# First eight weight slices in memory of their own, unit 0's scans ahead of them, and VectorE's and ScalarE's steps on attention results placed in the next half unit

## The chip, the cores and the metric

The kernel runs on one core of a Trainium2 chip. The engines are TensorE (PE, matmuls), VectorE (DVE), ScalarE (ACT), GpSimd (POOL) and SyncE (SP), which only issues transfers here. Each works through its own instructions in the order in which they were written. The metric is the device time of one execution in microseconds; a lower number is better. Each kernel is timed several times, and the median counts.

## What is computed

A recurrence over 768 positions for 4 x 8 heads of width 48, and two layers behind it:

```python
for t in range(S):
    cur = einsum('bhd,bhe->bhde', u[None] * k[t], v[t])
    y[t] = einsum('bhd,bhde->bhe', r[t], state + cur)
    state = w[t][..., None] * state + einsum('bhd,bhe->bhde', k[t], v[t])
x = y.transpose(0, 2, 1, 3).reshape(3072, 384)
x = ((x @ w1) * (x @ w2) @ w3) @ w_out          # 384 -> 1024 -> 384
h = x @ w_in                                    # 384 -> 2048
out = (h * clip(h + 3, 0, 6) / 6) @ w_out2      # 2048 -> 384
```

The weights come as 64-bit words and are made into float32 on the chip.

## The kernel before

**Attention** is cut into 32 *units* (a batch, one half of the positions, one pair of heads; `m` in the code). A unit is worked in *half units* k, two to a unit. In half 2m stand, in the kernel before, the transposes of k (`do_kn`) and the scores (`do_sc`) on TensorE, GpSimd's and VectorE's preparation of unit m+1 (`prep1`: two scans on VectorE, `e` and `f`, over its `wkr` tile), and at the half's end the mask (`do_mask`). In half 2m+1 stand `do_y(m-1)` and `do_kv(m)` on TensorE, `prep2(m+1)`, the load of unit m+2 (`wkr`, `rkv`; it takes the buffer that `do_y(m-1)` read), and at the end `do_x(m-1)` (VectorE's low part of y, transfers into `xt`), the state's scan and `prep3`. `do_y` ends with a copy on ScalarE. `kt` and `kvs` are ScalarE's copies out of PSUM for `do_kn` and `do_kv`. Three PSUM banks (`abank`) go round among all of these.

**Weights** come in 768 KB *slices*. A slice is loaded, converted in two passes on ScalarE (`a`) and two on VectorE (`b`); those for the first layer (`w12`) and later ones are also split into a high part (ScalarE) and a low part (VectorE) (`c`). `w3` and `w_out` are multiplied ahead of everything in twelve *turns*: turn i needs its own slice of `w3` and, in the first four, one of `w_out`. The matmuls of a turn are line 412; turns 0 to 7 have three groups of them, 8 to 11 two.

**The first layer** works on eight blocks of 384 tokens (`bi`), each in eight *slots* f: `ab(f, 0)` into bank 0, which ScalarE copies out, `ab(f, 1)` into bank 1, their product, the split into gh and gl, and `out1` of the slot before. The layer needs `xt` of the block, that is four units. `mm3` is three matmuls, of high with high, high with low and low with high parts.

**The order** is written out by hand: the engines follow the program's order. `burst(k)` puts the first part of half unit k into a turn or slot and `follow` the second. In the twelve turns half unit k stands in turn k+2. In the first block of the first layer (bi 0) ten half units, 10 to 19, stand in eight slots; f = 2 and f = 5 have two each. Then each slot has one.

Of the kernel before, what the change touches and what calls it, by code (L numbers as in the profile page):

```python
# [23 lines left out]
PR = 112  # L24
# [13 lines left out]
NH = 2 * NM + 2  # L38
# [5 lines left out]
def build(nc, tc, a):  # L44
# [80 lines left out]
    def load(m):  # L125
        wkr = att.tile([PR, WKR], F32, name=f"wkr_{m}", tag="wkr", bufs=3)
        nc.sync.dma_start(wkr, a["wkr"][m])
        rkv = att.tile([128, 3, NC, 2, D], F32, name=f"rkv_{m}", tag="rkv", bufs=3)
        nc.sync.dma_start(rkv, a["rkv"][m])
        un[m] = {"w": wkr[:, :WZ], "k": wkr[:, WZ:WZ + T1], "r": wkr[:, WZ + T1:], "rn": rkv[:, 0], "kn": rkv[:, 1],  # L130
                 "v": rkv[:, 2]}
# [97 lines left out]
    def do_y(m):  # L229
# [18 lines left out]
        y = att.tile([PR, 2, T1], F32R, name=f"y_{m}", tag="y")  # L248
        ACT.copy(y[:, 0], ps)
        d["y"] = y, ps  # L250

    def do_x(m):
        d = un.pop(m)
        b, h, p = m // (2 * NP), (m // NP) % 2, m % NP
        y, ps = d["y"]
# [10 lines left out]
    def attention():  # L266

        for m in range(NM + 1):
            if m < NM:
                do_kn(m)  # L270
                do_sc(m)
            if m + 1 < NM:
                prep1(m + 1)
# [4 lines left out]
            if m > 0:  # L278
                do_y(m - 1)
# [7 lines left out]
            if m > 0:  # L287
# [8 lines left out]
    at_half = [0]  # L296

    def burst(k):

        if at_half[0] == k < NH:  # L300
            next(steps)
            return True
        return False

    def follow(due):
        if due:
            next(steps)
            at_half[0] += 1


    class Slices:


        def __init__(self, bufs):
            self.args, self.raw, self.f, self.bufs, self.loaded = [], {}, {}, bufs, 0

        def load(self, upto):
            while self.loaded < min(upto, len(self.args)):
                key, n, src = self.args[self.loaded][:3]
                t = stg.tile([128, NW, 2], I32, name=f"raw_{key}", tag="raw")  # L320
                self.raw[self.loaded] = t
                nc.sync.dma_start(t[:, :n], src.bitcast(I32).rearrange("p (n t) -> p n t", t=2))
                self.loaded += 1

# [5 lines left out]
        def b(self, i):  # L330
            n, dst = self.args[i][1], self.args[i][3]
            conv_b(self.f[i], self.raw[i][:, :n], False)
            if dst is not None:
                self.load(i + self.bufs + 1)

        def c(self, i):
            dst, f = self.args[i][3], self.f.pop(i).bitcast(F32)
            if dst is not None:
                split(*dst, f)
                return  # L340
            parts = self.raw[i].rearrange("p n t -> p (n t)").bitcast(F32R).rearrange("p (t n) -> p t n", t=2)
            split(parts[:, 0], parts[:, 1], f)
            nc.sync.dma_start(w2d[i - SC], parts.bitcast(F32))
            self.load(i + self.bufs + 1)

    w12p = pool("w12p", bufs=1, side="left")
    w12h = w12p.tile([128, NF1, 2, KT, 128], F32R, name="w12h")
    w12l = w12p.tile([128, NF1, 2, KT, 128], F32R, name="w12l")
    ear = pool("ear", bufs=2, side="left")
    wo = ear.tile([128, NF1, DM], I32, name="wo", bufs=1)  # L350
    sl = Slices(3)
# [15 lines left out]
    sl.args += [(f"w12_{f}", NW, a["w12"][f], (w12h[:, f].rearrange("p s k m -> p (s k m)"),  # L367
                                               w12l[:, f].rearrange("p s k m -> p (s k m)"))) for f in range(NF1)]
# [420 lines left out]
```

## Time and profile before

| | |
|---|---|
| three runs | 926.89, 931.45 and 933.42 us; median 931.45 us |
| profiled execution | 924.55 us, of it 922.8 us from the first to the last instruction |
| TensorE matmuls busy | 866.3 us, 94% of the span |
| VectorE, ScalarE, GpSimd busy | 497.4, 381.0 and 153.0 us |
| mean granted clock of TensorE | 0.979 of full |

A profile is one execution, recorded instruction by instruction. A row of a timeline is an instruction or a run of like ones; behind it, in brackets, the time that the engine stood idle before it and what released it. The names are `output<-input`. L412 is a line of the kernel. TensorE counts two instructions for a matmul of float32 operands.

### The profile page before, as it was taken

To read this page: it belongs to the slowest core of one execution; us is meant where nothing else is said; L and a number is where in the kernel's file an instruction comes from. 1 tells how busy PE (TensorE), PEld (TensorE's weight loads), DVE (VectorE), ACT (ScalarE), POOL (GpSimd) and SP (SyncE) were. 2 spreads that over 40 slices of the span, in tenths; PEclk is the share of its full clock that TensorE was granted. 3 is DMA by queue.
4 is the path that set the end of the run, shared out by engine and by line. 5 is a ranking of instruction groups with operands and counts; after the bars stand their busy time and mean duration, and the time that the engine had idled before them with its cause. 6 is when DMAs were issued, how large, how long until landed. Compare 5 with 4: busy or idle time off the path is not lost.

```text
span 922.8 us, 13198 instructions
## 1 busy us (share of the span) xinstructions
PE 866.3 (94%) x5076; PEld 737.9 (80%) x5076; DVE 497.4 (54%) x783; ACT 381.0 (41%) x885; POOL 153.0 (17%) x186
## 2 busy tenths in 40 slices
PE   3886678999999999999999999999999999999997
PEld 1553567999999999989999788888888888888885
DVE  5876788668687687877433333433334334333332
ACT  4534554445544364444422433433333333333332
POOL 1323243225243443334000000000000000000000
PEclk9998788999999999999999999999999999999999
DMA  8746666255657466665279300100101100000001
GB/s 309 245 131 194 192 212 178 85 176 179 207 181 233 157 204 200 185 211 178 100 291 337 120 1 1 68 1 3 67 0 32 38 1 1 34 1 1 35 0 38
DMA packets 34727, 111.33 MB, mean 121 GB/s; under 512 B 4592, under 2 KB 8032, under 8 KB 34656
## 3 DMA queue, kind: packets, MB, share of 16 engines
q1 hardware_dynamic: 34656, 110.40, 37.1%
q8 instruction: 42, 0.69, 0.3%
q14 instruction: 29, 0.24, 0.1%
HBM read 78.92 MB, written 22.02 MB: 109 GB/s over the span
## 4 chain that ended last, share of the span: by engine, by line
PE 85%; DMA 5%; DVE 5%; issue 2%; ACT 2%; SPq 0%; DVEq 0%; ACTq 0%
PE bank L111 26%; PE bank L112 25%; PE bank L113 24%; PE abank L239 4%; DMA wkr<-in_wkr 3%; PE bank L412 2%; PE abank L194 2%; DMA raw_w<-in_w 1%; DMA xt<-y 1%; PE abank L210 1%; DVE w3f L103 1%; DVE e L146 1%; DVE w3f L104 1%; PE abank L183 1%; ACT sq L165 1%
## 5 line engine op out<-in xcount | busy, mean ns | idle before, releaser
L587 DVE SCALAR_TENSOR_TENSOR q<-q,bank 128x512 f32<-128x512 f32 x96 | 66.1, 688 | 195.2 <-ACT q L586 195.1
L586 ACT ACTIVATE q<-bank,half 128x512 f32<-128x512 f32 x96 | 66.3, 690 | 191.5 <-PE bank L113 191.4
L111 PE MATMUL bank<-xt,w12h 128*128 128x384 f32 x384 | 129.5, 337 | 7.3 <-DMA xt<-y 7.3
L113 PE MATMUL bank<-xt,w12l 128*128 128x384 f32 x384 | 129.0, 336 | 0.0
L112 PE MATMUL bank<-xt,w12h 128*128 128x384 f32 x384 | 128.9, 336 | 0.0
L112 PE MATMUL bank<-x,wih 128*128 128x512 f32 x288 | 114.9, 399 | 0.0
L112 PE MATMUL bank<-gl,w12h 128*128 128x512 f32 x288 | 113.9, 396 | 0.0
L111 PE MATMUL bank<-gh,w12h 128*128 128x512 f32 x288 | 113.7, 395 | 0.0
L111 PE MATMUL bank<-x,wih 128*128 128x512 f32 x288 | 113.5, 394 | 0.0
L113 PE MATMUL bank<-x,wil 128*128 128x512 f32 x288 | 112.8, 392 | 0.0
L113 PE MATMUL bank<-gh,w12l 128*128 128x512 f32 x288 | 112.6, 391 | 0.0
L108 DVE TENSOR_TENSOR gl<-q,gh 128x512 fp32r<-128x512 f32 x96 | 66.6, 693 | 65.5 <-ACT gh L107 65.5
L107 ACT CAST gh<-q 128x512 fp32r<-128x512 f32 x96 | 59.5, 620 | 65.6 <-DVE q L587 65.6
L412 PE MATMUL bank<-wo,w3f 128*128 128x384 f32 x128 | 53.8, 577 | 31.1 <-DVE w3f L104 29.5
L111 PEld LDWEIGHTS bank<-xt,w12h 128*128 128x128 f32 x384 | 72.7, 189 | 7.9 <-DMA xt<-y 7.7
L528 ACT CAST gh<-a 128x384 fp32r<-128x384 f32 x64 | 32.8, 513 | 111.3 <-DVE a L525 111.3
L525 DVE TENSOR_TENSOR a<-a,bank 128x384 f32<-128x384 f32 x64 | 35.3, 552 | 73.8 <-PE bank L113 71.4
L112 PEld LDWEIGHTS bank<-xt,w12h 128*128 128x128 f32 x384 | 72.7, 189 | 0.0
L113 PEld LDWEIGHTS bank<-xt,w12l 128*128 128x128 f32 x384 | 72.6, 189 | 0.0
L111 PE MATMUL bank<-gh,w34h 128*128 128x384 f32 x192 | 71.3, 372 | 0.6 <-ACT gh L528 0.6
L412 PEld LDWEIGHTS bank<-wo,w3f 128*128 128x128 f32 x128 | 27.5, 223 | 51.6 <-DVE w3f L104 31.3
L173 POOL TENSOR_SCALAR_AFFINE_SELECT A<-sd 128x384 f32<-128x384 f32 x64 | 50.0, 805 | 108.0 <-DVE sd L170 62.9
(101 smaller groups left out, 1491.2 us busy)
## 6 DMA issues: line engine op xcount, KB each, us to landing
wkr<-in_wkr SPq DMA_DIRECT2D x32, 505.8 KB, 5.5
rkv<-in_rkv SPq DMA_DIRECT2D x32, 432.0 KB, 6.3
raw_w<-in_w SPq DMA_DIRECT2D x16, 768.0 KB, 4.9
xt<-y SPq DMA_DIRECT2D x48, 144.0 KB, 5.2
raw_w_in<-in_w_in SPq DMA_DIRECT2D x8, 768.0 KB, 5.0
w2d<-raw_w_in SPq DMA_DIRECT2D x8, 768.0 KB, 3.3
raw_w_out<-in_w_out SPq DMA_DIRECT2D x8, 768.0 KB, 4.9
w2d<-raw_w_out SPq DMA_DIRECT2D x8, 768.0 KB, 3.3
```

Of the source, the lines that this page charges most:

```text
L107: ACT.copy(hi, src)
L108: (eng or V).tensor_tensor(out=lo, in0=src, in1=hi.bitcast(F32), op=ALU.subtract)
L111: mm(ps, wh, xh, start=first, stop=False)
L112: mm(ps, wh, xl, start=False, stop=False)
L113: mm(ps, wl, xh, start=False, stop=last)
L173: P_.affine_select(out=A[:, j], in_=sd[:, :, j].unsqueeze(2).to_broadcast([128, NC, C]), pattern=[[0, NC], [-1, C]], compare_op=ALU.is_equ ...
L239: mm(pc[rows[j], c], left, right, start=not started[j], stop=True, skip_group_check=True)
L412: mm(bank[g % 5][:, :DM], w3[:, j, g - g0], wo[:, 2 * jp + j].bitcast(F32), start=jp + j == 0, stop=jp == NF1 // 2 - 1 and j == 1)
L525: V.tensor_tensor(out=at, in0=at, in1=bank[1][:, :T1], op=ALU.mult)
L528: ACT.copy(gh, at)
L586: ACT.activation(q, ps, AF.Relu, bias=half, scale=1.0 / 6.0)
L587: V.scalar_tensor_tensor(out=q, in0=q, scalar=1.0, in1=ps, op0=ALU.min, op1=ALU.mult)
```

## The change

1. The first eight slices (`w_out` 0 to 3 and `w3` 0 to 3) get tiles of their own (`homes`), in the memory in which the first layer's weights `w12h` and `w12l` are made at turn 9. All eleven slices up to `w3` 6 are asked for at the start. The converted `wo` and `w3f` tiles move to the other side of the memory.
2. Unit 0's `wkr` is loaded first of all and its scans are put ahead of the first slice. Slice 1 and the constants are issued from ScalarE's queue.
3. A half unit now begins with `follow(k)`, which holds what works on TensorE's results of the half before: at the start of half 2m the copy of y, `do_x(m-2)` and the state's scan of unit m-1, at the start of half 2m+1 the mask of unit m. `prep3` moves to half 2m. There are 67 half units instead of 66.
4. Half unit k stands in turn k+1 instead of k+2. In the first block nine half units, 11 to 19, stand in eight slots, two of them in f = 3.
5. The high part of a split slice is cast behind its conversion (`b`) instead of with the low part; the low parts of the first two `w12` slices come a turn later. In a turn, the passes of `a` stand ahead of `b`.

```diff
     def attention():
 
-        for m in range(NM + 1):
+        for m in range(NM + 2):
+            if m > 1:
+                do_x(m - 2)
+            if 0 < m <= NM:
+                do_state(m - 1)
+            yield
             if m < NM:
                 do_kn(m)
                 do_sc(m)
+            if 0 < m < NM:
+                prep3(m)
             if m + 1 < NM:
                 prep1(m + 1)
             yield
             if m < NM:
                 do_mask(m)
             yield
...
-            if m > 0:
-                do_x(m - 1)
-            if m < NM:
-                do_state(m)
-            if m + 1 < NM:
-                prep3(m + 1)
-            yield
...
+    def follow(k):
         if at_half[0] == k < NH:
             next(steps)
+            at_half[0] += 1
+
+    def burst(k):
+        follow(k)
+        if at_half[1] == k < NH:
             next(steps)
-            at_half[0] += 1
+            at_half[1] += 1
...
                 key, n, src = self.args[self.loaded][:3]
-                t = stg.tile([128, NW, 2], I32, name=f"raw_{key}", tag="raw")
+                if self.loaded < len(self.homes):
+                    t = self.homes[self.loaded]
+                else:
+                    t = stg.tile([128, NW, 2], I32, name=f"raw_{key}", tag="raw")
...
             if dst is not None:
...
+            ACT.copy(dst[0], self.f[i].bitcast(F32))
...
+    load(0, 0)
+    ACT.dma_start(d1c, a["d1c"])
     sl.load(2)
-    nc.sync.dma_start(d1c, a["d1c"])
-    load(0)
+    load(0, 1)
     for nm, t in (("u", ub), ("ident", ident), ("mask", mask)):
-        nc.sync.dma_start(t, a[nm])
-    sl.load(3)
+        ACT.dma_start(t, a[nm])
+    sl.load(4)
     load(1)
+    sl.load(len(homes) + 3)
...
         for f in range(NF1):
+            k = NF1 * bi + f + LEAD - (bi == 0 and f < 4)
+            if bi or f:
+                follow(k)
...
-            k = NF1 * bi + f + LEAD - (2 if f < 3 else 1 if f < 6 else 0) * (bi == 0)
-            due = burst(k)
+            burst(k)
```

The copy of y also moves in the code, from the end of `do_y` to the start of `do_x`.

**SyncE's queue at the start.** `home` and `raw_w3` are slices, `wkr` and `rkv` are what a unit loads. Before:

```order
L322 DMA raw_wo_1_131<-in_w_out 128x1536
L127 DMA wkr_1_133<-in_wkr 112x1156
L129 DMA rkv_1_135<-in_rkv 128x864
L322 DMA raw_w3_1_156<-in_w3 128x1536
L322 DMA raw_wo_2_160<-in_w_out 128x1536
L322 DMA raw_w3_2_183<-in_w3 128x1536
L322 DMA raw_wo_3_187<-in_w_out 128x1536
L322 DMA raw_w3_3_216<-in_w3 128x1536
L322 DMA raw_w3_4_220<-in_w3 128x1536
L322 DMA raw_w3_5_254<-in_w3 128x1536
L322 DMA raw_w3_6_258<-in_w3 128x1536
L127 DMA wkr_2_288<-in_wkr 112x1156
```

After:

```order
L329 DMA home2_115<-in_w_out 128x1536
L329 DMA home3_116<-in_w3 128x1536
L128 DMA wkr_1_137<-in_wkr 112x1156
L132 DMA rkv_1_139<-in_rkv 128x864
L329 DMA home4_117<-in_w_out 128x1536
L329 DMA home5_118<-in_w3 128x1536
L329 DMA home6_119<-in_w_out 128x1536
L329 DMA home7_120<-in_w3 128x1536
L329 DMA raw_w3_4_145<-in_w3 128x1536
L329 DMA raw_w3_5_147<-in_w3 128x1536
L329 DMA raw_w3_6_149<-in_w3 128x1536
L128 DMA wkr_2_273<-in_wkr 112x1156
```

The slices that waited for a buffer now stand in one row, and unit 2's `wkr` behind eleven of them (one is issued from ScalarE).

**ScalarE, turn 5 before and turns 4 and 5 after.** `w3f_7` and `w3f_6` are the slices of the turn after next, `y_0` the copy of unit 0's result. Before:

```order
L249 CAST y_0_363<-abank2_69 112x384
L215 COPY kvs1_99<-abank0_67 112x48x3
L162 COPY pb0_100<-e_2_332 112x48x3
L165 ACTIVATE sq_2_0_376,stat_74<-wkr_2_288 112x128
L165 ACTIVATE sq_2_1_378,stat_74<-wkr_2_288 112x128
L165 ACTIVATE sq_2_2_380,stat_74<-wkr_2_288 112x128
L94 ACTIVATE w3f_7_390,sums_77<-raw_w3_7_294 128x768
L96 ACTIVATE raw_w3_7_294<-raw_w3_7_294 128x768
L185 COPY kt_2_414<-abank1_68 128x336
L148 COPY stat_74<-d1v1_97 112x3
```

After:

```order
L217 COPY kvs1_99<-abank0_67 112x48x3
L164 COPY pb0_100<-e_2_311 112x48x3
L167 ACTIVATE sq_2_0_359,stat_74<-wkr_2_273 112x128
L167 ACTIVATE sq_2_1_361,stat_74<-wkr_2_273 112x128
L167 ACTIVATE sq_2_2_363,stat_74<-wkr_2_273 112x128
L94 ACTIVATE w3f_6_369,sums_77<-raw_w3_6_149 128x768
L96 ACTIVATE raw_w3_6_149<-raw_w3_6_149 128x768
L257 CAST y_0_382<-abank2_69 112x384
L187 COPY kt_2_394<-abank1_68 128x336
L150 COPY stat_74<-d1v1_97 112x3
```

The copy of y has moved behind kvs, pb, the squares and the two passes over a slice.

**TensorE, first block of the first layer.** `abank` are the banks of attention; before, in slot f = 2, where units 5 and 6 meet (the same stands at f = 5 for units 7 and 8):

```order
L183 MATMUL abank0_67<-ident_73,wkr_6_662 128x112 x2
L194 MATMUL abank1_68<-wkr_6_662 128x128
L194 MATMUL abank2_69<-wkr_6_662 128x128
L194 MATMUL abank1_68<-wkr_6_662 128x128
L194 MATMUL abank2_69<-wkr_6_662 128x128
L194 MATMUL abank1_68<-wkr_6_662 128x128
L194 MATMUL abank2_69<-wkr_6_662 128x128
L239 MATMUL abank0_67<-wkr_5_568,s_5_821 48x128 x6
L239 MATMUL abank0_67<-A_5_680,rkv_5_570 48x128 x6
L210 MATMUL abank1_68<-rkv_6_664,kt_6_870 48x48 x4
```

After, in slot f = 3, where units 6 and 7 meet:

```order
L185 MATMUL abank2_69<-ident_73,wkr_7_779 128x112 x2
L196 MATMUL abank0_67<-wkr_7_779 128x128
L196 MATMUL abank1_68<-wkr_7_779 128x128
L196 MATMUL abank0_67<-wkr_7_779 128x128
L196 MATMUL abank1_68<-wkr_7_779 128x128
L196 MATMUL abank0_67<-wkr_7_779 128x128
L196 MATMUL abank1_68<-wkr_7_779 128x128
L241 MATMUL abank2_69<-wkr_6_647,s_6_941 48x128 x6
L241 MATMUL abank2_69<-A_6_837,rkv_6_649 48x128 x6
L212 MATMUL abank0_67<-rkv_7_781,kt_7_977 48x48 x4
```

Two places at which half units stand directly behind one another have become one.

## Rows read from the trace of the kernel before

**Rows 1.** Windows; columns: length, busy us of each engine (instructions), clock, DMA share, GB/s

```profile
105.92:173.40 67.48, 58.10 (x438) 53.38 (x439) 50.65 (x82) 30.88 (x88) 18.62 (x23) 0.87 0.51 152
...
155.00:460.00 305.00, 302.54 (x2378) 284.28 (x2375) 223.13 (x372) 146.19 (x430) 108.39 (x128) 0.99 0.57 176
```

**Rows 2.** What TensorE waited for; columns: us in total, times, longest us

```profile
PE bank L412 <- DVE w3f L104: 29.5, 7, 11.2
PE bank L111 <- DMA xt<-y: 7.3, 1, 7.3
PE abank L239 <- ACT kt L185: 5.8, 2, 3.3
```

**Rows 3.** Chain that ended last, stretch 49 to 65 us; start, us, what

```profile
54.52 3.88 DMA wkr<-in_wkr
...
58.49 0.98 DVE e L146
...
61.55 0.97 DVE w3f L104
```

**Rows 4.** DMA issues: KB each, median us to landing

```profile
wkr<-in_wkr SPq DMA_DIRECT2D x32, 505.8 KB, 5.5
...
raw_w<-in_w SPq DMA_DIRECT2D x16, 768.0 KB, 4.9
```

**Rows 5.** Windows over the first 20 us, columns as in Rows 1

```profile
0.00:10.00 10.00, 0.00 (x0) 0.00 (x0) 4.97 (x9) 4.85 (x7) 1.54 (x10) 1.00 0.80 263
10.00:20.00 10.00, 7.11 (x12) 3.64 (x12) 5.28 (x7) 2.69 (x6) 2.89 (x2) 1.00 1.03 366
```

**Rows 6.** Timeline of ScalarE; start us, us, instruction, [idle before <-releaser]

```profile
55.33 0.48 ACT L249 CAST y<-abank 112x384 fp32r<-112x384 f32 x1 [7.00 <-PE abank L239]
...
55.70 0.29 ACT L215 COPY kvs<-abank 112x144 f32<-112x144 f32 x1
...
58.17 0.90 ACT L96 ACTIVATE raw_w<-raw_w 128x768 int32<-128x768 uint8 x1
...
100.73 0.82 ACT L107 CAST w12h<-f_w 128x768 fp32r<-128x768 f32 x1
```

**Rows 7.** Timeline of VectorE, columns as in Rows 6

```profile
55.84 0.56 DVE L256 TENSOR_TENSOR y<-abank,y 112x384 fp32r<-112x384 f32 x1 [2.42 <-ACT y L249]
...
56.88 0.43 DVE L170 TENSOR_REDUCE sd<-rkv 128x6 f32<-128x288 f32 x1
...
101.58 0.96 DVE L108 TENSOR_TENSOR w12l<-f_w,w12h 128x768 fp32r<-128x768 f32 x1 [1.41 <-ACT w12h L107]
```

**Rows 8.** Timeline of TensorE, turns 4, 5, 9 and 10

```profile
39.76 2.85 PE L412 MATMUL bank<-wo,w3f 128*128 128x384 f32 x8
...
49.74 4.14 PE L412 MATMUL bank<-wo,w3f 128*128 128x384 f32 x12 [2.81 <-DVE w3f L104]
...
55.11 0.44 PE L210 MATMUL abank<-rkv,kt 128*48 128x48 f32 x12
...
77.22 5.26 PE L412 MATMUL bank<-wo,w3f 128*128 128x384 f32 x8 [4.91 <-DVE w3f L104]
...
84.08 2.85 PE L412 MATMUL bank<-wo,w3f 128*128 128x384 f32 x8
```

**Rows 9.** Windows behind the two waits for kt, and one at full clock

```profile
126.11:133.49 7.38, 6.15 (x42) 5.26 (x43) 7.31 (x13) 4.16 (x14) 3.24 (x3) 0.54 0.76 244
...
142.65:146.14 3.49, 3.49 (x42) 3.29 (x42) 2.84 (x6) 1.95 (x8) 0.00 (x0) 1.00 0.36 117
...
153.12:160.76 7.64, 6.04 (x46) 5.27 (x46) 6.67 (x12) 3.00 (x11) 4.27 (x6) 0.55 0.79 240
```

**Rows 10.** Timelines of ScalarE, VectorE and TensorE in one slot

```profile
181.20 0.48 ACT L523 COPY a<-bank 128x384 f32<-128x384 f32 x1 [1.08 <-PE bank L113]
...
181.93 0.96 DVE L104 SCALAR_TENSOR_TENSOR f_w_in<-raw_w_in,f_w_in 128x768 int32<-128x768 int32 x1
...
186.00 0.33 PE L111 MATMUL bank<-xt,w12h 128*128 128x384 f32 x1
```

More of the change, by code (lines that the diff above doesn't have):

```diff
@@ L123, in psum_a, with load @@
         return abank[nbank[0] % 3]
[L125 to L131, printed above, removed]
+    def load(m, part=None):
+        if part != 1:
+            wkr = att.tile([PR, WKR], F32, name=f"wkr_{m}", tag="wkr", bufs=3)
+            nc.sync.dma_start(wkr, a["wkr"][m])
+            un[m] = {"w": wkr[:, :WZ], "k": wkr[:, WZ:WZ + T1], "r": wkr[:, WZ + T1:]}
+        if part != 0:
+            rkv = att.tile([128, 3, NC, 2, D], F32, name=f"rkv_{m}", tag="rkv", bufs=3)
+            nc.sync.dma_start(rkv, a["rkv"][m])
+            un[m].update(rn=rkv[:, 0], kn=rkv[:, 1], v=rkv[:, 2])
     def c3(x):
@@ L247, in do_y @@
                 part(j, c, d["v"][:, c, j], d["A"][:, j, c])
[L248 to L250 removed]
+        d["y"] = ps
     def do_x(m):
@@ L254, in do_x @@
         b, h, p = m // (2 * NP), (m // NP) % 2, m % NP
-        y, ps = d["y"]
+        ps = d["y"]
+        y = att.tile([PR, 2, T1], F32R, name=f"y_{m}", tag="y")
+        ACT.copy(y[:, 0], ps)
         V.tensor_tensor(out=y[:, 1], in0=ps, in1=y[:, 0].bitcast(F32), op=ALU.subtract)
@@ L366, in build @@
     S12 = len(sl.args)
-    sl.args += [(f"w12_{f}", NW, a["w12"][f], (w12h[:, f].rearrange("p s k m -> p (s k m)"),
-                                               w12l[:, f].rearrange("p s k m -> p (s k m)"))) for f in range(NF1)]
+    sl.args += [(f"w12_{f}", NW, a["w12"][f], f) for f in range(NF1)]
     SC = len(sl.args)
@@ L397, in w34_part @@
             split(w34h[:, g], w34l[:, g], bank[g % 5][:, :DM])
+    w12 = []
+    prep1(0)
     for q in of[0]:
@@ L421, in build @@
         else:
-            burst(i - 2)
+            burst(i - 1)
+        if i + 2 < len(turns):
+            for q in of[i + 2]:
+                sl.a(q)
+        if i == 9:
+            close("hm")
+            w12p = pool("w12p", bufs=1, side="left")
+            w12 += [w12p.tile([128, NF1, 2, KT, 128], F32R, name=f"w12{x}") for x in "hl"]
+        if i >= 9:
+            sl.a(S12 + i - 9)
         if i + 1 < len(turns):
@@ L427, in build @@
             sl.b(S12 + i - 10)
-        if i + 2 < len(turns):
-            for q in of[i + 2]:
-                sl.a(q)
-        if i >= 9:
-            sl.a(S12 + i - 9)
-        follow(i > 1)
-        if i >= 10:
-            sl.c(S12 + i - 10)
+        if i >= 11:
+            sl.c(S12 + i - 11)
+    sl.c(S12 + 1)
     w34_part((6, 7))
     close("ear")
+    w12h, w12l = w12
     x1p = pool("x1p", bufs=1, side="left")
@@ L538, in build @@
                 step += 1
-            follow(due)
-            if bi == 0 and f in (2, 5):
-                follow(burst(k + 1))
+            if bi == 0 and f == 3:
+                burst(k + 1)
             if prev is not None:
@@ L544, in build @@
             prev = bi, f, gh, gl
-            if bi == 6 and at_half[0] == NH and "h" not in p2:
+            if bi == 6 and at_half[1] == NH and "h" not in p2:
                 win_start()
```

56 lines of the change are left out of this document (30 added, 26 removed).

## Prediction

> **What bounds the kernel now.** I read first the busy time by stage [rows 1]. From 155 to 460 us TensorE works 302.5 of 305 us, so in the long middle no wait is left for a change of order to remove. In the first layer's first block of tokens (105.9 to 173.4 us) it works 58.1 of 67.5 us, and part of that at a low clock. So what can be won lies before 173 us. Then I read who made TensorE wait [rows 2]: the converted weight slices of the twelve turns (29.5 us in 7 waits), the one transfer of attention output into `xt` ahead of the first layer (7.3 us) and ScalarE's copy of `kt` (two waits, 5.8 us), which is where two half units stand directly behind one another. These three are what the change touches. The rest of this part of the program is a chain over two turns: matmuls of turn i, `do_y` and `do_kv` behind them, then either a load of `wkr` or ScalarE's work, then VectorE's two scans and its conversion of the slice for turn i+2, then the matmuls of turn i+2 [rows 3].
>
> The sum is made against the profiled execution, 924.55 us (span 922.8 and 1.75 around it). It is 6.9 us below the median of the runs shown (931.45), and they spread over 6.5 us; so a difference under about 1% (9.3 us) is hardly told from none here.
>
> **Up to turn 4.** Slices now wait for no buffer until the twelfth, so the queue is full from the start, and bytes decide. Ahead of unit 2's `wkr` now stand eleven slices of 768 KB, two earlier `wkr` [rows 4], and by their shapes 0.9 MB of `rkv` and 0.5 MB of constants; with `wkr` 2 itself that is 8.65 + 1.55 + 0.9 + 0.5 = 11.6 MB. The transfers moved 263 GB/s in the first 10 us and 366 GB/s in the next 10 [rows 5]. At these rates 2.6 MB are there at 10 us and the other 9.0 MB take 24.5 us: `wkr` 2 lands at 34.5 us. Behind it VectorE runs unit 2's scans and the conversion of turn 4's slice. In the trace from the scan at 58.49 to the end of the conversion at 62.5 this is 4.0 us [rows 3]. So turn 4 starts at 38.5 us; before it was 39.8 [rows 8]. VectorE itself doesn't set it: by then it has 9 slices at 1.95, three pairs of scans at 2.1 and some 4 us of smaller work, 28 us from about 5 on. The scans of unit 0 ahead of the first slice cost their 2.1 us at the first matmul alone and are caught up in that wait. If the queue kept 263 GB/s, `wkr` 2 would land at 44.2; I take 366, the row of the ten microseconds in which the queue was as full as it now will be. So up to here the gain is 1.3 us, but the attention stands one half unit further.
>
> **From turn 4 to the first layer.** The order on VectorE is cyclically the old one. On ScalarE it isn't: `do_x`'s copy of y stood ahead of kvs, pb and squares; now it stands behind them and behind the first pass over the slice of turn i+2. So x, the state scan, the reduction and the next scans wait for it. By rows, a new loop over two turns is: matmuls, y and kv 5.8 (49.74 to 55.55) [rows 8]; to ScalarE 0.2; kvs, pb, squares and the slice 3.4 (55.70 to 59.07), y 0.5 [rows 6]; from x to the end of the reduction 1.5 [rows 7]; scans and conversion 4.0. That is 15.4 us. The old loop went over the load (3.9 us from 54.52) [rows 3] and took 12.8 at the same place: the new one is 2.5 us longer. Turns 4 to 6 and 6 to 8 cost 15.4 each. Turns 8 to 10 have two groups of matmuls instead of three (2.85 us instead of 4.14) [rows 8]: 14.1. Slices there are a third narrower too; what that saves I leave uncounted, against conversions that run longer beside GpSimd's work. From turn 10 to the first layer the conversion's high part (0.8) [rows 6] and low part (0.9) [rows 7] of the first w12 slice come on top: 15.8. Together 60.7 us. In each loop TensorE has work for about 11 of 15 us, so one wait of some 4 us is left per loop. A wait of 2.81 us left the twelve matmuls behind it at 4.14 us, which is full speed; one of 4.91 us was followed by 5.26 us where 2.85 is usual [rows 8]. The new waits are nearer to the second, so I add 2.4 us for each of three loops, 7.2.
>
> The Trainium skill (TensorE: Matmul & The Clock Gate, section "HAM oscillation — how this bites in real kernels") tells of a loop in which one wait per turn drops the clock so that every turn starts at the lower level, and advises another order of the loop. The two rows bear that out for the longer wait and not for the shorter; by that rule all three loops pay and the sum stays, by the row of 2.81 us none pays and the end would be 7.2 us earlier. It speaks against this change, which gathers the waits.
>
> So the first layer's third matmul, the first that needs the low part, comes at 38.5 + 60.7 + 7.2 = 106.4. Before, six matmuls ran ahead of the wait for `xt` and the seventh came at about 105.9. Now four more matmuls stand behind it, 0.7 us. The wait for `xt` (7.3) is gone, since y of unit 3 is out one turn earlier, but what is late next is that low part on VectorE. Net: 1.2 us later than before.
>
> **The first block of the first layer.** Before, unit 6's two halves stand directly behind one another and unit 8's again: the half with `do_y` must wait for `kt`, `do_kv` for the mask. The two waits for `kt` are 5.8 us [rows 2]; in the stretches behind them TensorE stood another 1.23 and 1.60 us (7.38 less 6.15, 7.64 less 6.04), and its granted clock was 0.54 and 0.55 of full, nearly always the lower of its two levels (1.2 of 2.4 GHz) [rows 9]. Work of the same kind at full clock takes 3.49 us there, so the clock cost 2.7 and 2.5 us. In all 13.8 us for two places. After the change one such place is left, at f = 3. I cost it at half, 6.9, and win 6.9. The half unit that moved ahead of the layer takes about 1 us of matmuls with it; against it stands that ScalarE's copy of bank 0 now queues behind the cast of the high part, which waits for VectorE. I set these two against each other. VectorE keeps up: it was busy 50.7 of 67.5 us [rows 1] and gets one half unit less.
>
> **Later.** The half units run one place earlier or later beside the same tiles, and TensorE is full; the end of attention is tied to the same y, so layer 2 finds its weights as before. I count nothing.
>
> Sum: 1.2 - 6.9 = -5.7 us, 919 in a profile like the one shown, and 931.45 - 5.7, about 926, beside the median.
>
> **Rivals.**
> - *The gathered waits are cheap.* If they come out under 3 us, the clock stays up: 7.2 us less, -12.9, 918.6. For it: the row of 2.81; narrower slices shorten the last loops. Against it: the sum leaves about 4 us.
> - *The front is late.* All early transfers now share the engines at once; if they move 310 GB/s on average instead of 366, `wkr` 2 lands at 39 and turn 4 starts at 43. Nothing later takes up those 4.5 us, as the loops are chains. -1.2 us, 930. For it: only one ten-microsecond row shows 366. Against it: that row is the fullest.
> - *Slower: the cast in front of bank 0.* In every slot that converts a slice (6 in the first block, 16 later), ScalarE's cast of the high part now stands ahead of the copy that frees bank 0, and waits for VectorE's conversion. In the slot at 180 us the copy ran at 181.20, the conversion ended at 182.89, and bank 0 was needed again at 186.00 [rows 10]. The copy would now end at 182.9 + 0.8 + 0.5 = 184.2, 1.8 us in time. From a conversion that ends over 1.8 us later on TensorE waits, microsecond for microsecond, where it now never does. At 1 us in each of 22 slots this is +22, so +16 in all: 948. For it: VectorE is busy 223 of 305 us there [rows 1], and its work comes in lumps. Against it: the slack, which grows in slots without a lump.
> - *Another double place instead.* If the place at f = 3 costs as much as both did (as masks now stand ahead of it), the sum is +1.2: 933.
>
> **Chances.** Forecast (-9 to -2) 0.48; cheap waits 0.22; late front 0.15; double place 0.07; cast 0.08. Faster by over 1% (below 922.1) takes most of the cheap waits and the forecast's lower edge: 0.33. Slower by over 1% (above 940.8) is the cast: 0.08. The rest, 0.59, is within 1%. The range reaches from the cheap waits with a good front (-17, 914) to the late front or the double place (933), and leaves out the cast and the tail below.
>
> **What would show it.** First matmul at 13 to 14 us instead of 11.2; turn 4 near 39 us with unit 2's scans released by its `wkr`; from turn 4 on VectorE idle ahead of x, released by ScalarE's copy of y, 4 to 6 us a time; waits of TensorE of about 4 us before turns 6, 8 and 10 with a low granted clock behind them; no wait for `xt`, but one for the low part of the first slice; one wait for `kt` instead of two. It would be wrong if turn 4 came after 43 us, if bank 0 appeared among TensorE's waits after 175 us, or if the loops took no longer than 13 us.

## The result, and the profile after

The changed kernel takes 920.49 us (median of 4 runs, 918.39 to 920.89), the kernel before beside it 929.39 (4 runs, 926.89 to 933.42): ratio 0.9896, 95% interval 0.9851 to 0.9940. The forecast was 926 with a range of 914 to 933. The profiled execution took 918.39 us with a span of 916.7, against 924.55 and 922.8 before: 6.1 us less, where the sum had said 5.7. The medians are further apart, 8.9 us: in the twenty executions of the kernel before that were timed beside E1 to E4, time and granted clock go together (924.58 us at 0.979, 934.80 us at 0.967), and the profiled one (924.55 us at 0.979) is among the shortest. So the account below explains the 6.1 us of two profiles; where the other 3 us of the medians lie isn't shown. The first tile of the second block of tokens, (1,0), begins at 166.76 instead of 173.38, 6.6 us earlier, and from there to the end the changed kernel takes 749.9 us and the one before 749.4. So all of the 6.1 us was won ahead of 167 us, as forecast; but the steps didn't each give what the sum said.

What TensorE waited for, after (us in total, times, longest):

```profile
PE bank L436 <- DVE w3f L104: 29.3, 7, 16.5
PE bank L113 <- DVE w12l L363: 4.2, 1, 4.2
PE abank L241 <- ACT kt L187: 4.1, 1, 4.1
PE abank L196 <- DVE y L258: 2.9, 2, 2.1
PE bank L111 <- ACT a L553: 2.2, 2, 1.9
PE abank L212 <- DVE A L202: 2.0, 4, 0.8
```

Beside [rows 2], the wait for `xt` (7.3) is gone, and one wait for `kt` is left instead of two. New are the low part of the first w12 slice (4.2) and bank 0, which ScalarE's copy frees too late (2.2); the wait for VectorE's part of y, 0.7 before, is 2.9. The converted slices cost as much as before, 29.3 against 29.5, though 16.5 of it is now the start.

Rows picked from the timeline of TensorE after: the first matmul, turns 4, 6, 8, 10, the third matmul of the first layer, and two places in the first block:

```profile
16.53 10.44 PE L436 MATMUL bank<-wo,w3f 128*128 128x384 f32 x24 [16.53 <-DVE w3f L104]
39.78 4.14 PE L436 MATMUL bank<-wo,w3f 128*128 128x384 f32 x12
55.00 5.83 PE L436 MATMUL bank<-wo,w3f 128*128 128x384 f32 x12 [2.80 <-DVE w3f L104]
70.93 2.85 PE L436 MATMUL bank<-wo,w3f 128*128 128x384 f32 x8 [3.20 <-DVE w3f L104]
83.87 5.49 PE L436 MATMUL bank<-wo,w3f 128*128 128x384 f32 x8 [3.56 <-DVE w3f L104]
102.67 0.69 PE L113 MATMUL bank<-xt,w12l 128*128 128x384 f32 x1 [4.23 <-DVE w12l L363]
125.38 0.44 PE L111 MATMUL bank<-xt,w12h 128*128 128x384 f32 x1 [1.93 <-ACT a L553]
134.03 1.52 PE L241 MATMUL abank<-wkr,s 48*48 48x128 f32 x12 [4.09 <-ACT kt L187]
```

Windows after, columns as in [rows 1]: the first block, the double place, and the matmuls of turns 6, 10 and 8:

```profile
102.67:166.76 64.09, 56.76 (x428) 51.36 (x428) 52.49 (x81) 31.98 (x91) 23.10 (x23) 0.91 0.55 171
134.03:141.50 7.47, 6.64 (x43) 5.71 (x44) 6.67 (x12) 3.20 (x13) 5.24 (x5) 0.54 0.56 177
55.00:60.83 5.83, 5.83 (x14) 3.00 (x14) 4.19 (x6) 0.00 (x0) 1.53 (x3) 0.71 0.27 90
83.87:89.36 5.49, 5.49 (x10) 2.59 (x11) 5.42 (x8) 1.00 (x3) 1.95 (x3) 0.50 0.40 143
70.93:73.78 2.85, 2.85 (x10) 1.51 (x12) 2.85 (x7) 0.00 (x1) 1.53 (x3) 1.00 0.50 171
```

Read both together: turn 6 at a granted clock of 0.71 and turn 10 at 0.50, the lower level, pay 1.7 and 2.6 us over the 4.14 and 2.85 of full clock. Turn 8, behind a wait between the two in length, pays nothing in this execution; in E2 and E4 below it does.

VectorE after: the first conversion, the scan that opens unit 2, and the four places where it waits for y:

```profile
11.58 0.96 DVE L103 SCALAR_TENSOR_TENSOR wo<-wo,home 128x768 int32<-128x768 int32 x1 [2.73 <-ACT home L96]
35.33 0.96 DVE L148 TENSOR_TENSOR_SCAN e<-wkr,d1c 112x388 f32<-112x388 f32 x1
49.36 0.56 DVE L258 TENSOR_TENSOR y<-abank,y 112x384 fp32r<-112x384 f32 x1 [2.51 <-ACT y L257]
65.82 0.56 DVE L258 TENSOR_TENSOR y<-abank,y 112x384 fp32r<-112x384 f32 x1 [6.59 <-ACT y L257]
78.76 0.56 DVE L258 TENSOR_TENSOR y<-abank,y 112x384 fp32r<-112x384 f32 x1 [3.30 <-ACT y L257]
95.56 0.56 DVE L258 TENSOR_TENSOR y<-abank,y 112x384 fp32r<-112x384 f32 x1 [6.11 <-ACT y L257]
```

The scan at 35.33 has no idle time before it: `wkr` 2 was there, and from 11.58 to 39.5 VectorE runs without a gap. The last four rows are the stall that the prediction put into its loops. ScalarE after, from the matmuls' end to y, and the cast in front of bank 0's copy:

```profile
62.55 0.28 ACT L217 COPY kvs<-abank 112x144 f32<-112x144 f32 x1 [8.71 <-PE abank L212]
...
64.78 0.65 ACT L96 ACTIVATE raw_w<-raw_w 128x512 int32<-128x512 uint8 x1
65.33 0.46 ACT L257 CAST y<-abank 112x384 fp32r<-112x384 f32 x1
...
124.12 0.83 ACT L355 CAST w12h<-f_w 128x768 fp32r<-128x768 f32 x1 [4.06 <-DVE f_w L104]
124.86 0.47 ACT L553 COPY a<-bank 128x384 f32<-128x384 f32 x1
```

Between the matmuls' end (62.5) and the copy of y (65.33) ScalarE does 2.8 us of other work, while VectorE stands; of the 6.59 us that it stood, about half fall into this time, and the rest ahead of the matmuls' end. And the cast at 124.12 waited 4.06 us for VectorE with the copy of bank 0 behind it.

### The profile page after: what moved, and what is told of

Its sections match the earlier page's. It is cut to its first block, busy times and chain, and to the rows that moved or that the text cites. A ratio compares the mean times of both kernels' runs of the same rounds, so it can differ in the third digit from the quotient of the medians.

```text
span 916.7 us, 13158 instructions
## 1 busy us (share of the span) xinstructions
PE 863.8 (94%) x5076; PEld 736.0 (80%) x5076; DVE 497.9 (54%) x783; ACT 380.6 (42%) x885; POOL 173.3 (19%) x186
## 4 chain that ended last, share of the span: by engine, by line
PE 85%; DVE 7%; ACT 3%; DMA 3%; issue 1%; SPq 0%; DVEq 0%; ACTq 0%
PE bank L111 26%; PE bank L112 25%; PE bank L113 24%; PE abank L241 5%; PE abank L196 2%; PE bank L436 2%; DMA wkr<-in_wkr 2%; DMA home<-in_w 1%; PE abank L212 1%; DVE e L148 1%; ACT sq L167 1%; DVE w3f L103 1%; PE abank L185 1%; DVE A L202 1%; DVE f_w L104 1%
## 5 line engine op out<-in xcount | busy, mean ns | idle before, releaser
L175 POOL TENSOR_SCALAR_AFFINE_SELECT A<-sd 128x384 f32<-128x384 f32 x64 | 84.0, 1334 | 146.1 <-DVE sd L172 70.8
L436 PE MATMUL bank<-wo,w3f 128*128 128x384 f32 x128 | 51.0, 554 | 29.4 <-DVE w3f L104 29.3
L112 PE MATMUL bank<-gl,w34h 128*128 128x384 f32 x192 | 65.0, 339 | 0.5 <-DVE gl L560 0.5
```

What stands on the lines that cost most here:

```text
L112: mm(ps, wh, xl, start=False, stop=False)
L175: P_.affine_select(out=A[:, j], in_=sd[:, :, j].unsqueeze(2).to_broadcast([128, NC, C]), pattern=[[0, NC], [-1, C]], compare_op=ALU.is_equ ...
L436: mm(bank[g % 5][:, :DM], w3[:, j, g - g0], wo[:, 2 * jp + j].bitcast(F32), start=jp + j == 0, stop=jp == NF1 // 2 - 1 and j == 1)
```

## The experiments

Every kernel of the experiments was timed in five rounds beside the kernel before; the ratios are against it (that of the changed kernel is the one above). "Low part" is the start of the first layer's third matmul (before, and in E3, where the wait stands at `xt`: the matmul behind that wait), (1,0) the start of the second block's first tile ("half unit (1,0)" in the expectations), all in us of one profiled execution each.

```
kernel                          turn 4  low part   (1,0)   span   ratio (95% interval)
before                           39.76   105.92   173.38   922.8
after                            39.78   102.67   166.76   916.7  0.9896 (0.9851 to 0.9940)
E3  front alone                  36.67   103.58   170.76   920.6  0.9963 (0.9943 to 0.9983)
E2  without homes                41.13   104.53   169.57   918.9  0.9938 (0.9912 to 0.9963)
E1  y early                      39.55    94.60   159.29   909.0  0.9798 (0.9769 to 0.9827)
E4  double place later           40.70   104.04   168.11   917.1  0.9893 (0.9863 to 0.9923)
E8  matmuls in the waits         39.20    99.46   164.56   914.1  0.9840 (0.9806 to 0.9873)
E5  y early, cast late           39.26    96.89   156.37   906.5  0.9751 (0.9716 to 0.9787)
E6  y early, one queue           37.86    94.69   159.35   909.7  0.9802 (0.9764 to 0.9840)
E9  y early, low part first      39.48    91.58   159.68   908.9  0.9795 (0.9759 to 0.9831)
E10 four edits                   40.78    95.02   155.45   905.6  0.9736 (0.9704 to 0.9768)
E11 E10, low part first, xt      38.85    90.53   154.34   904.5  0.9736 (0.9711 to 0.9761)
E14 y early, double at f = 6     39.77    94.97   158.71   909.5  0.9783 (0.9761 to 0.9806)
E15 E11, double at f = 6         37.75    89.58   152.20   902.6  0.9713 (0.9684 to 0.9742)
```

From (1,0) to the end of the span all fourteen lie between 749.0 and 750.8 us: whatever is won stands at (1,0).

**E3, front alone, and E2, without homes.** E3 is the kernel before with the front of the change (homes, unit 0's scans first, ScalarE's queue). 

> The kernel before with the front of the change alone: eight slices into the first layer's memory, unit 0's scans first, slice 1 and the constants from ScalarE's queue; the half units stay where they were, with y's copy in do_y. Theory (the gain sits in the first block, where one double place is left instead of two): turn 4 starts at 39 to 41 us as in both kernels, since VectorE sets it; the two waits for kt (5.8 us) and the wait for xt (7.3 us) stay; the first block begins and ends as before, 167 to 175 us for half unit (1,0); time against the kernel before 0.995 to 1.003, that is, of the gain of 1.0% at most a half. Rival (the front is what wins, since no loop waits for a load of wkr any more): each of the loops is 2 to 4 us shorter than before, the first layer begins 6 us or more earlier, ratio 0.985 to 0.992.

E2 is the changed kernel without the homes:

```
-    homes = [hm.tile([128, NW, 2], I32, name=f"home{q}") for q in range(8)]
+    homes = []
...
-    sl.load(4)
+    sl.load(3)
     load(1)
-    sl.load(len(homes) + 3)
```

and with the second passes of turn i+1 ahead of the first passes of turn i+2. 

> The changed kernel with its half units where the change places them, but without the eight slices in the first layer's memory: three buffers as before, and each turn's first pass ahead of the one after it, as the buffers need it. Theory (the placement wins in the first block; the front only keeps the loads away from the loops): the loops wait for wkr again, up to 4 us in one or two of them, the third matmul of the first layer comes 2 to 6 us later than in the changed kernel (102.7), from there to half unit (1,0) it takes 62 to 65 us as in the changed kernel; ratio against the kernel before 0.990 to 0.998. Rival (the front wins, the placement gives nothing): 0.998 to 1.005. Second rival (the slices in the first layer's memory give nothing at all): 0.988 to 0.991, as the changed kernel.

At (1,0) E3 wins 2.6 us on before and E2 3.8: together 6.4, and the change has 6.6. Both keep unit 0's scans first and ScalarE's queue, so the split isn't clean, but neither half needs the other. The placement looks the larger; the intervals of the two ratios overlap. In E3 turn 4 comes at 36.67, not at 39 to 41 as expected: there the attention is a half unit less far and VectorE has less ahead of it. Its waits for `xt` (6.7) and `kt` (two, 5.8 in all) stay as in [rows 2]. In E2 the loops do not wait for `wkr` again, against the expectation; from turn 4 to the low part they take 63.4 us, as after (62.9). By one profile each, the homes, with that order of passes, are worth 1.35 us at turn 4 and 2.8 at (1,0); 1.5 of the 2.8 is turn 8, which ran at the lower clock in E2 (4.39 us instead of 2.85), and by ratio E2 and the changed kernel aren't told apart.

**E1, y early.** The copy goes back to the end of `do_y`, and `do_x` takes both tiles from there:

```
-        d["y"] = ps
+        y = att.tile([PR, 2, T1], F32R, name=f"y_{m}", tag="y")
+        ACT.copy(y[:, 0], ps)
+        d["y"] = y, ps
...
-        ps = d["y"]
-        y = att.tile([PR, 2, T1], F32R, name=f"y_{m}", tag="y")
-        ACT.copy(y[:, 0], ps)
+        y, ps = d["y"]
```

> The changed kernel with ScalarE's copy of y back at the end of do_y, as before the change; all else as changed. Theory (the copy of y behind kvs, pb, squares and a slice's pass lengthens each loop over two turns, and TensorE pays in waits before turns 6, 8 and 10 and in the lower clock behind them): VectorE's idle time ahead of x falls from 2.5 to 6.6 us to under 1.5 us a time, the loops shrink by 1 to 3 us each, the third matmul of the first layer comes 4 to 8 us before 102.7; ratio against the kernel before 0.981 to 0.986. Rival (something else is late next in the loop: kvs and pb, which now stand behind the copy, or the slices on VectorE): the loops stay within 0.5 us each, ratio 0.988 to 0.991. Second rival (the copy waits for the last matmuls of do_y and holds ScalarE's queue): slower than the changed kernel, 0.991 to 0.996.

The low part comes 8.1 us earlier and the span is 7.7 us shorter, more than expected. E1's VectorE and TensorE, where after had 6.59 and 6.11 idle, 15.93 between turns 6 and 8, and 18.80 from turn 10 to the low part:

```profile
60.07 0.56 DVE L258 TENSOR_TENSOR y<-abank,y 112x384 fp32r<-112x384 f32 x1 [2.42 <-ACT y L251]
...
85.68 0.56 DVE L258 TENSOR_TENSOR y<-abank,y 112x384 fp32r<-112x384 f32 x1 [1.50 <-ACT y L251]
```

```profile
53.97 4.14 PE L436 MATMUL bank<-wo,w3f 128*128 128x384 f32 x12 [2.00 <-DVE w3f L104]
67.01 2.85 PE L436 MATMUL bank<-wo,w3f 128*128 128x384 f32 x8 [2.00 <-DVE w3f L104]
79.18 4.54 PE L436 MATMUL bank<-wo,w3f 128*128 128x384 f32 x8 [3.67 <-DVE w3f L104]
94.60 0.69 PE L113 MATMUL bank<-xt,w12l 128*128 128x384 f32 x1 [4.36 <-DVE w12l L363]
```

The four stretches from turn 4 to the low part are 14.42, 13.04, 12.17 and 15.42 us, against 15.22, 15.93, 12.94 and 18.80: the place of one copy of 0.46 us cost the changed kernel 7.8 us, through VectorE's idle time and, at turns 6 and 10, through the clock.

**E8, matmuls in the waits.** It asks whether the clock is a cost of its own:

```
         w3 = w3s.pop(i).bitcast(F32).rearrange("p (j g m) -> p j g m", j=2, m=128)
+        for q in range(6 if i in (6, 8, 10) else 0):
+            mm(bank[3 if i == 10 else 2][:, :DM], wo[:, 0, :128].bitcast(F32), wo[:, 1].bitcast(F32), start=True, stop=True)
```

> The changed kernel with six more matmuls ahead of turns 6, 8 and 10 each, whose results nobody reads: they stand in the places where TensorE waits 2.8, 3.2 and 3.6 us for a converted slice, and fill 2.1 us of each (six of 0.35 us). Nothing else is changed. Theory (the lower clock behind those waits is a cost of its own, beside the wait): turns 6 and 10 run at 4.14 and 2.85 us instead of 5.83 and 5.49, the third matmul of the first layer comes 2 to 5 us before 102.7; ratio against the kernel before 0.984 to 0.988. Rival (the low clock costs nothing, since VectorE and ScalarE set the loop and the next wait only grows): turns 6 and 10 at full speed, but the next waits longer by as much, 0.988 to 0.991. Second rival (the fillers delay the slices' matmuls or don't keep the clock): 0.989 to 0.995.

```profile
55.55 4.03 PE L438 MATMUL bank<-wo,w3f 128*128 128x384 f32 x12
70.38 2.74 PE L438 MATMUL bank<-wo,w3f 128*128 128x384 f32 x8
83.56 2.74 PE L438 MATMUL bank<-wo,w3f 128*128 128x384 f32 x8
```

All three turns run at full clock (granted 1.00). One such matmul is two instructions, so six took 4.14 us and not 2.1: turn 6 now starts 16.35 us behind turn 4 instead of 15.22. Yet the low part comes 3.2 us earlier, 0.6 of which is from ahead of turn 4; the other 2.6 are the clock's, net of that delay. So the low clock is a cost beside the wait. Matmuls that compute nothing paid for themselves, though six were more than the waits held.

**E4, the double place later.**

```
-            if bi == 0 and f == 3:
-                burst(k + 1)
             if prev is not None:
                 out1(*prev)
+            if bi == 0 and f == 3:
+                burst(k + 1)
```

> The changed kernel with the second half unit of f = 3 in the first block placed behind out1 of the tile before instead of ahead of it. Theory (the last double place costs its wait for kt of 4.1 us, 0.8 us for the mask and the low clock behind): the wait for kt falls under 1 us, the stretch from the third matmul to half unit (1,0) shrinks by 2 to 5 us; ratio against the kernel before 0.984 to 0.988. Rival (what comes behind it is late anyway, or the pair of out1 and half unit now delays bank 0's product): the stretch stays within 1 us, ratio 0.988 to 0.991.

```profile
135.35 0.90 PE L241 MATMUL abank<-wkr,s 48*48 48x128 f32 x12 [0.85 <-ACT kt L187]
...
139.15 0.56 PE L212 MATMUL abank<-rkv,kt 128*48 128x48 f32 x8 [2.11 <-DVE A L202]
```

The wait for `kt` fell from 4.09 to 0.85, and the one for the mask grew from 0.83 to 2.11; from the low part to (1,0) it is 64.07 us, after 64.09. The wait fell as the theory said, but the stretch stayed, as the rival said: a wait was moved, nothing won.

**E5, the cast behind bank 0's copy**, on E1. In the slots of the first layer that convert a slice, `b` leaves the cast out and the slot does it behind the copy:

```
             ACT.copy(at, bank[0][:, :T1])
+            if bi == 0 and f + 2 < NF1:
+                sl.high(S12 + f + 2)
+            elif bi and step < 3 * NF2 and step % 3 == 1:
+                sl.high(SC + step // 3)
             ab(f, 1, x)
```

> The changed kernel with y's copy early (0.980 of the kernel before), and with ScalarE's cast of a slice's high part behind its copy of bank 0 instead of ahead of it, in every slot of the first layer that converts a slice. Theory (ahead of the copy, the cast waits for VectorE and holds bank 0: TensorE's wait of 1.9 us in the first block is its cost, and later there is slack): that wait goes, ratio 0.977 to 0.979 if nothing else is late, the long middle unchanged. Rival (VectorE's own lateness is the cause, the wait only goes to the next operation, gh or the low part): 0.979 to 0.982. Second rival (the cast in front costs in later slots too): under 0.976.

The wait for bank 0 is gone, and the first block shrinks by more than that wait: from the low part to (1,0) 59.48 us instead of E1's 64.69. Its low part came 2.3 us later than E1's, with turns 8 and 10 at the lower clock, so 2.9 of these 5.2 us reach (1,0). The later low part isn't what shortens the block: from the start of tile f = 1 to that of f = 5, the seven kernels with the cast in front and the double place at f = 3 take 37.11 to 38.76 us, whenever their low part comes, and E5, E10 and E11, with the cast behind, 33.55 to 34.49. The ratio is the one of the second rival (under 0.976), but not for its reason. E1 and E5 take the same from (1,0) on (749.7 and 750.1): in the later slots the cast in front costs nothing.

**E6, one queue**, on E1: `nc.sync` instead of `ACT` issues slice 1, d1c and the constants. 

> The changed kernel with y's copy early (0.980 of the kernel before), and with slice 1, d1c and the constants issued from SyncE's queue in the same order as before the change of queue, ScalarE issuing none. Theory (VectorE is busy without a gap from 11.6 us to turn 4, so the start of its first slice sets turn 4, and the transfer of d1c and slice 1 on a second queue takes bandwidth from slice 0): slice 0 lands 1 to 2.5 us earlier, the first matmul comes at 13.5 to 15.5 instead of 16.3, turn 4 at 37.5 to 39 instead of 39.6, and the end by as much: ratio 0.9775 to 0.979. Rival (turn 4 waits for something else as well, or the loops take it up at a load of wkr): first matmul earlier, end the same, 0.979 to 0.981. Second rival (one queue is slower, as SyncE issues one after another): first matmul later than 16.3, over 0.981.

The first rival's ratio came out, but not its cause. The first pass over slice 0 starts at 7.27 instead of 9.56, the first matmul comes at 13.99 instead of 16.29 and turn 4 1.7 us earlier. No load takes that up: turn 6 still starts 2.4 us ahead of E1's. Then turns 6 and 8 fall to the lower clock (granted 0.71 and 0.62), which no rival had named, and give it back:

```profile
51.58 5.83 PE L436 MATMUL bank<-wo,w3f 128*128 128x384 f32 x12 [1.88 <-DVE w3f L104]
...
65.81 4.54 PE L436 MATMUL bank<-wo,w3f 128*128 128x384 f32 x8 [1.50 <-DVE w3f L104]
```

**E9, the low part first**, on E1: `sl.c(S12 + i - 11)` moves ahead of `sl.b(S12 + i - 10)`. 

> The changed kernel with y's copy early (0.980 of the kernel before), and with the low part of the first w12 slice ahead of the conversion of the second on VectorE, in the last turn. Theory (TensorE's wait of 4.4 us for the low part is VectorE's order: the part's input is there at 89.6 us, but scans of 2.5 us and a conversion of 2.4 us stand ahead of it): the third matmul of the first layer comes at 92 to 92.7 instead of 94.6; then xt (0.3 us behind in the run before) or the second tile is next, so of the 2.2 us some 1 to 2 reach the end: ratio 0.978 to 0.979. Rival (the conversion that is now later delays the second tile by as much): 0.9795 to 0.981.

```profile
91.58 0.44 PE L113 MATMUL bank<-xt,w12l 128*128 128x384 f32 x1 [1.57 <-DVE w12l L363]
96.30 0.66 PE L111 MATMUL bank<-xt,w12h 128*128 128x384 f32 x1 [3.60 <-DMA xt<-y]
```

The wait for the low part fell from 4.36 to 1.57, and `xt`, hidden behind it until then, is late next with 3.60; (1,0) doesn't move. The rival's ratio came out, though what ate the gain was `xt` and not the second tile.

**E10, four edits; E11, two more.** E10 joins E1, E5, E6 and fewer matmuls in the waits, `range({6: 2, 8: 2, 10: 4}.get(i, 0))`. 

> The changed kernel with four edits together: y's copy early, the cast behind bank 0's copy, one queue for the first transfers, and matmuls without a reader in the waits of turns 6, 8 and 10, fewer than in the run with fillers alone (two of 0.69 us at turns 6 and 8, four at turn 10, as the waits with y early are 1.5 to 2.1 and 3.7 to 4.0 us). Theory (with the clock kept up, the 1.7 us that one queue gave at turn 4 and the 1.7 us of the cast reach the end): turn 4 at 37.5 to 38.2, turns 6, 8 and 10 at 4.14, 2.85 and 2.85 us, half unit (1,0) begins 3 to 5 us before 159.3, ratio 0.970 to 0.975 against 0.980 with y early alone. Rival (the loops are set by loads of wkr and by VectorE, the end stays): 0.975 to 0.979. Second rival (the fillers delay the turns): over 0.979.

Turns 6, 8 and 10 run at 4.14, 2.85 and 2.85. Turn 4 came later than expected, since VectorE here waited 1.83 us for unit 2's `wkr`:

```profile
35.89 0.97 DVE L148 TENSOR_TENSOR_SCAN e<-wkr,d1c 112x388 f32<-112x388 f32 x1 [1.83 <-DMA wkr<-in_wkr]
```

With VectorE started earlier, that transfer is next, though not by as much in every execution: E6, E11 and E15, with the same front, waited 0.28, 0.64 and 0.27 us there. Turn 4 itself ran at the lower clock (granted 0.71, 5.83 us). The profiled execution, 907.39 us, is 2.5 us above the median of its six runs, so the late turn 4 need not be in all of them. The ratio is as the theory said, but E5 alone has 0.9751: what one queue and the matmuls in the waits add to it isn't told from nothing.

E11 adds E9's edit and, for the last unit of the first `xt`, `(ACT if m == NP - 1 else nc.sync).dma_start`. 

> As the kernel with four edits, and two more: the low part of the first w12 slice ahead of the conversion of the second, and the last two transfers of y into the first xt issued from ScalarE's queue instead of SyncE's. Theory (with the low part early, TensorE waited 3.6 us for xt in the run before; that transfer took 9.4 us from its issue because 2.5 MB of loads stood ahead of it on its queue): on a queue of its own it lands in 4 to 6 us, the wait for xt falls under 1 us, and 2 to 4 us more reach half unit (1,0): ratio 0.966 to 0.972. Rival (all queues share the same engines, the transfer takes as long as before): the wait stays 2 to 4 us and the end that of the four edits. Second rival (ScalarE waits for y's low part on VectorE and holds the next operations): later than with four edits.

Transfers of y into `xt` (KB each, median us to landing), in E9 and then in E11, from 78 and 76 to 100 us:

```profile
xt<-y SPq DMA_DIRECT2D x2, 144.0 KB, 9.4
```

```profile
xt<-y ACTq DMA_DIRECT2D x2, 144.0 KB, 6.5
```

The transfer is shorter (in E10, on SyncE's queue, it took 8.5 us), if not the 4 to 6 us of the theory, and `xt` is waited for no more. In its place stand the low part again (3.85) and bank 0, which is read out for the last `w34` blocks (2.35). (1,0) comes 1.1 us earlier than in E10, and the ratio is that of E10, as the first rival had it.

**E14, the double place at f = 6**, on E1, and **E15**, the same on E11. 

> The changed kernel with y's copy early (0.980 of the kernel before), and the one remaining double place moved from f = 3 to f = 6 of the first block, behind the last conversion of a slice. Theory (the double place costs what it costs because VectorE has a slice's conversion between its two halves, so that mask, kt and the next y come late): at f = 6 the waits for kt and the mask are under 2 us in all instead of 4.7, the clock stays up, the stretch from the third matmul to half unit (1,0) shrinks by 2 to 5 us of its 64.7; ratio 0.974 to 0.978. Rival (two half units behind one another always cost about 5 us, wherever they stand): the stretch within 1 us of 64.7, 0.979 to 0.981. Second rival (unit 7's x now comes too late for the second block): a wait for xt at (1,0) of some us, 0.979 to 0.985.

> As the kernel with the four edits, the low part first and xt from ScalarE's queue (0.974 of the kernel before), with the double place moved from f = 3 to f = 6 as well. Theory (at f = 6 the wait for kt went, but ScalarE's copy of bank 0, behind a cast that waits for VectorE, took its place with 4.6 us; with the cast behind the copy that isn't there): no wait for kt, bank 0's waits under 0.5 us, the stretch from the third matmul to half unit (1,0) is 59 to 61.5 us instead of 63.8, ratio 0.969 to 0.972. Rival (VectorE's conversions and half units set the stretch, so another operation is late in their place): 62.5 to 64.5 us, ratio 0.973 to 0.975.

```
-            k = NF1 * bi + f + LEAD - (bi == 0 and f < 4)
+            k = NF1 * bi + f + LEAD - (bi == 0 and f < 7)
...
-            if bi == 0 and f == 3:
+            if bi == 0 and f == 6:
```

E14's waits for bank 0, which were 1.9 us in E1:

```profile
PE bank L111 <- ACT a L553: 4.6, 3, 1.9
```

The wait for `kt` is gone (3.9 in E1), and bank 0 took its place; from the low part to (1,0) it is 63.74, 1 us less, as the first rival had it; the ratio lies between the two ranges. In E15 neither is there; the mask (1.6), y (1.4) and the scanned `wkr` (0.9) are, each a VectorE product, and the stretch is 62.62, as the rival said. The ratio is in the theory's range; the time, 903.72, isn't told from E11's 904.28. E15 is faster than both the kernel before and the changed one.

## Why the prediction was right

**The start.** First matmul: 13 to 14 us said, 16.53 measured. Slice 0 landed at 9.80, as slice 1 and d1c from ScalarE's queue moved beside it; E6 puts them on one queue and has 13.99. Turn 4: 38.5 said, 39.78 measured, so the step was nearly right in time and wrong in cause. It said "bytes decide" and put VectorE at "28 us from about 5 on"; but VectorE starts its first conversion at 11.58 and then has no gap. E6, which starts it earlier, moves turn 4 by 1.7. That the two reckonings end within 1.3 us of each other is luck. The rival of a late front (turn 4 at 43) did not come, though E10 shows that `wkr` 2 lies close behind.

**From turn 4 to the low part** the sum had 60.7 + 7.2 = 67.9 us; it took 62.9. The clock was charged three times at 2.4; turns 6 and 10 paid 1.7 and 2.6 and turn 8 nothing, 4.3 instead of 7.2. Turn 8 doesn't always go free: E2 and E4 paid there as well (4.39 and 4.41 us instead of 2.85). The waits were 2.80, 3.20 and 3.56 us, not "about 4". Without these shares the four loops took 15.2, 14.2, 12.9 and 16.2 us, against 15.4, 15.4, 14.1 and 15.8 in the sum: the two loops between turns 6 and 10 are each over 1 us shorter than said. That is the narrower slices, which the sum left uncounted: against the loop before them, ScalarE takes 2.8 us instead of 3.2 from kvs to the copy of y, and VectorE 5.1 instead of 5.6 from the low part of y to the end of the conversion. The loop of 12.94 us is just under the 13 us that were to count against the prediction, the other three well over it, and the mechanism was right: VectorE stood 2.5 to 6.6 us ahead of x at ScalarE's copy of y (4 to 6 said), and E1 takes that away and wins 7.8 us. Instead of 1.2 us behind the kernel before, the changed one is here 2.5 ahead (after 0.7 for four matmuls).

**The first block** is the step that failed to the other side: 6.9 us of gain said, about 61 us from the low part to (1,0), 64.1 measured. The one double place costs 4.09 + 0.83 us of waits and about 2.8 of low clock (6.64 us busy, of it 0.33 for the next tile, against 3.49 at full clock [rows 9]), in all 7.7 instead of 6.9. What was mis-sized above all is the cast in front of bank 0's copy, which the prediction set off against a half unit's matmuls, and which it priced as a rival for all 22 slots by the slack of one later slot (at 180 us). In the later slots it costs nothing: after 170 us TensorE never waits for ScalarE's copy of bank 0, so this sign against the prediction did not come. In the first block it costs 1.93 at 125.38 and more behind it: E5 takes it away, and tiles f = 1 to 4 take 33.55 us instead of 37.66 in E1.

So two errors cancelled: the prediction had the low part 3.7 us too late and the first block 2.8 us too short. The steps and their direction were mostly right, but that 6.1 us came out for 5.7 is luck. The rival of cheap waits had its condition wrong both ways: the wait under 3 us (2.80) was followed by the lower clock, the one of 3.20 by the full. The rival of a double place at the price of both is out (7.7 us, not 13.8), and E4 and E14 show why such a place is hard to buy off: VectorE is busy 52.5 of the block's 64.1 us, and behind each wait taken away stands its next product. That this is the whole bound of the block is argued, not shown.

The Trainium skill ("TensorE: Matmul & The Clock Gate", section "HAM oscillation — how this bites in real kernels") describes such a loop with a low clock behind each wait. Here it holds for two loops of three in the changed kernel's profile and for all three in E2's and E4's, and E8 shows the price.

## What to carry to other kernels

When an order is moved on several engines at once, ask of each step who stands still for it: a copy of 0.46 us placed behind work that nobody waits for cost about as much as the whole change won (E1 against the changed kernel, 7.7 us of span; the change, 6.1 by the profiles and 8.9 by the medians). A wait taken off a chain is worth something only up to the next product in line, so read that one's time before counting the gain. Where TensorE waits in a loop, the clock behind the wait can be a cost of its own, and matmuls without a reader can be cheaper than idling.

## What the hardware showed that I had not expected

In these runs the length of a wait doesn't tell the clock behind it. Waits of 1.50 and 1.88 us (E6), 2.80 and 3.56 (after) were followed by slow turns; waits of 2.00 twice (E1), 2.81 [rows 8] and 3.20 (after) by full speed. Turn 8 shows it best: 3.20 us of wait and full speed in the changed kernel, and the same turn behind nearly the same wait at a granted clock of 0.63 in E2 and in E4:

```profile
72.29 4.39 PE L435 MATMUL bank<-wo,w3f 128*128 128x384 f32 x8 [3.21 <-DVE w3f L104]
```

```profile
71.79 4.41 PE L436 MATMUL bank<-wo,w3f 128*128 128x384 f32 x8 [3.18 <-DVE w3f L104]
```

What else decides, these runs don't settle.

VectorE's conversion of 768 columns takes 0.96 us alone and up to 1.55 beside GpSimd. The changed kernel's GpSimd, and its VectorE at the same time:

```profile
11.68 1.52 POOL L144 TENSOR_TENSOR rkv<-rkv 128x288 f32<-128x288 f32 x1 [9.41 <-DMA rkv<-in_rkv]
13.28 1.39 POOL L145 TENSOR_TENSOR rkv<-rkv,ub 128x288 f32<-128x288 f32 x1
```

```profile
12.57 1.44 DVE L104 SCALAR_TENSOR_TENSOR wo<-home,wo 128x768 int32<-128x768 int32 x1
13.94 1.55 DVE L103 SCALAR_TENSOR_TENSOR w3f<-w3f,home 128x768 int32<-128x768 int32 x1
15.52 0.96 DVE L104 SCALAR_TENSOR_TENSOR w3f<-home,w3f 128x768 int32<-128x768 int32 x1
```

GpSimd's two operations end at 13.20 and 14.67; VectorE's passes that begin inside them are long, the next one is short again. GpSimd's are long too: the second operation takes 0.81 us at 40.28, where VectorE stands, and 1.39 here. The Trainium skill ("SBUF — State Buffer", section "SBUF: two separate sides") has the two engines share a pair of ports that one holds for a whole instruction. The trace agrees to within 0.15 us: 0.96 us from GpSimd's ends at 13.20 and 14.67 gives 14.16 and 15.63, and the passes ended at 14.01 and 15.49.

Two queues shared the bandwidth of the first transfers: slice 0's first pass, released by its transfer, started at 9.56 in E1 and at 7.27 with one queue (E6).

```profile
9.56 0.89 ACT L94 ACTIVATE wo<-home 128x768 f32<-128x768 f32 x1 [1.37 <-DMA home<-in_w_out]
```

```profile
7.27 0.89 ACT L94 ACTIVATE wo<-home 128x768 f32<-128x768 f32 x1 [0.22 <-DMA home<-in_w_out]
```

The Trainium skill ("DMA: Bandwidth & Descriptors", section "Queues, rings and completion order") has the transfer engines take turns between queues; this agrees.
